# A decode layer's forward heads by pairs: 2 MB cache loads, half-array sums and a shorter softmax loop

## The chip, the cores and the metric

The kernel runs on one core of a Trainium2 chip. The metric is the device time of one execution in microseconds (us): the median of the runs, 1684.61 us for the kernel before (three runs, 1684.12 to 1685.03). A core has five engines that work from their own queues: TensorE (PE; its weight loads are shown as PEld), VectorE (DVE), ScalarE (ACT), GpSimd (POOL) and SyncE (SP), which here issues nearly all the DMAs. Sixteen DMA engines move the data.

## The reference

One decode layer, forward and backward. With B = 4, H = 32, Sk = 4096, Dh = 128, D = 512, F = 1792, all bf16:

```
q   = layernorm(x) @ wq                      # [B, H, 1, Dh]
p   = softmax(q @ k_cache^T / sqrt(Dh))      # [B, H, 1, Sk]
o   = p @ v_cache
h   = x + o @ wo
out = h + (silu(ln(h) @ w1) * (ln(h) @ w3)) @ w2
returned: out and the gradients of x, k_cache, v_cache, wq, wo, w1, w3, w2 for a given grad_out
```

There are 128 heads (batch times head). Each has a K and a V of 4096 x 128 bf16, 1 MB each, so each cache holds 134 MB. The forward part reads both, the backward part reads V again and writes gradients of the size of both.

## The kernel before, in words

**Memory.** One arena of 23 slots of 1 MB (128 partitions x 8320 bytes) holds everything large. `Slot` takes a free one, `give` returns it to the end of the free list. A load into a slot is issued by SP at its place in the program, and waits there for whoever used the slot last.

**Forward part** (to about 665 us). A head's K lies as [partition p, 32 rows j, 128]: partition p holds 32 neighbouring positions, 8 KB. The loop at the end of the diff runs over 64 groups `gi` of G = 2 heads, a = 2 gi and a + 1. The order in each engine's queue is the order of the program text. In one group:

- `S_head` (L393): scores of both heads into one PSUM tile of 128 x 256. Heads take different rows, and quarters c of the array's columns work on quarters of the sequence.
- `sm_max`, `sm_max_T`, `sm_gmax`, `sm_bcast`, `sm_exp`, `sm_sum`, `sm_norm`, `sm_P`: the softmax. The maximum over a row on VectorE (mx, L400), a mask that puts -1e30 in rows of the other head (mxm, L402), a transpose on PE (x_ps, L407), the maximum for each head (gm, L412), its broadcast back by a matmul (b_ps, L417), a copy to SBUF on VectorE (nm, L422), the exponential on ACT (L425), the sum over rows by a matmul (l_ps, L431), the reciprocal (rl, L436), the scaling on ACT (Pn, L439), eight transposes (pt_P, L446) and four copies into P_all (L450).
- For the next group, K is transposed: a quarter on PE with a copy on ACT (`T_pe`, L361, L362), three quarters on VectorE (`T_dve`, L367). POOL prepares W, the masked queries (`q_stationaries`, L373).
- `PK_pairs` (POOL, L456) and `PK_mul` (VectorE, L460): the product of K with the head's probabilities, into a slot PK with two extra columns that hold p itself.
- `M_mm` (L475): 32 steps of a full-array matmul, lhsT = V rows, rhs = PK rows (130 columns), summed over positions in PSUM. It gives the head's output o and a 128 x 128 matrix that the backward part uses for the gradient of q. It runs two to three heads behind, in pieces between the softmax steps: m1 = a - 3 and m2 = a - 2.
- `M_end` (L485, L489): the sums of PK over positions for 32 heads collect in one PSUM tile kP; the head's M is copied by ACT into a slot that holds 16 heads and stays taken until the backward part.
- `kP_flush` after every 32nd head: an ACT copy of kP (L496), four products (L499) and a copy (L500), at once. `O_cols` after every 16th head: two small VectorE copies of the outputs (L505, L507).

K is loaded up to seven heads ahead (`more_K`), V three (`load_V`), each by one DMA of 1 MB. In the last groups `weights` loads the middle part's weights with what slots are left (`reserve`).

**Middle part** (to about 720 us): the rest of the layer forward, and backward to the gradient of o. **Backward part**: heads 0 to 31 one by one, heads 32 to 127 by 48 pairs. A pair is two heads of one batch entry, s and s + 4, in one DMA of 2 MB: partitions 0 to 63 hold the first head, 64 to 127 the second, 64 positions (16 KB) in each partition. The outer products for the gradients of K and V are at L820 and L1434. The probabilities, which the forward part leaves in the layout of single heads, are regrouped for pairs by PE and ACT (`P_rows`).

Of the kernel before, what the change touches and what calls it, by code (L numbers as in the profile page):

```python
# [15 lines left out]
G = 2  # L16
VQ = 3
# [7 lines left out]
LEAD = 64  # L25


@with_exitstack
def kernel(
# [81 lines left out]
    part = {"B": False, "side_done": False}  # L111
# [14 lines left out]
    class Slot:  # L126
        def __init__(self, name, src=free):
            self.i = src[0]
            if part["B"] and src is free:
                lone = sorted((i for i in free if i not in part["pairs"]), key=age, reverse=True)  # L130
                self.i = lone[0] if name in SIDE or lone and age(lone[0]) >= OLD else max(free, key=age)
# [44 lines left out]
    Ks, Vs, KTs, PKs = {}, {}, {}, {}  # L176

    def load_K(s):
        if s < NH:
            Ks[s] = Slot("Kn")  # L180
            nc.sync.dma_start(out=Ks[s].heads(), in_=cache_head(A_k_cache, s))

    nvl = {"n": 0}

    def load_V(s):
        if s < NH and s >= nvl["n"]:
            nvl["n"] = s + 1
            Vs[s] = Slot("Vn")
            nc.sync.dma_start(out=Vs[s].heads(), in_=cache_head(A_v_cache, s))


    def more_K(s):
        while len(Ks) + kdone["n"] < min(NH, s + 8) and len(free) > 1:
            load_K(len(Ks) + kdone["n"])

    kdone = {"n": 0}
    more_K(0)
# [6 lines left out]
    ones_f = const.tile([P, P], FP32, name="ones_f")  # L204
    nc.gpsimd.memset(ones_f[:], 1.0)
# [10 lines left out]

    def ones_window(col):
        i = col % 2
        return onesw[i][:, 32 - i - col:64 - i - col]
# [3 lines left out]
    rowg = fcon.tile([P, 8], FP32, name="rowg")  # L223
    nc.vector.tensor_reduce(out=rowg[:], in_=ident_f.rearrange("p (c g q) -> p g c q", c=4, q=4), axis=AX.XY, op=ALU.add)
    quad = fcon.tile([P, 4], FP32, name="quad")
    nc.vector.tensor_reduce(out=quad[:], in_=ident_f.rearrange("p (q i) -> p q i", q=4), axis=AX.X, op=ALU.add)
    bsum = fcon.tile([P, P], FP32, name="bsum")
    nc.vector.tensor_copy(out=bsum.rearrange("p (c g q) -> p c g q", c=4, q=4),
                          in_=rowg[:, None, :, None].to_broadcast([P, 4, 8, 4]))
    maskneg = fcon.tile([P, G], FP32, name="maskneg")  # L230
    nc.vector.tensor_scalar(out=maskneg[:], in0=rowg[:, 0:G], scalar1=-1.0, scalar2=1e30, op0=ALU.add, op1=ALU.mult)
    wmask = fcon.tile([P, G, 32], BF16, name="wmask")
    nc.gpsimd.memset(wmask[:], 0.0)
    for g in range(G):
        nc.vector.tensor_copy(out=wmask[:, g, 4 * g:4 * g + 4], in_=quad[:])
    selg = fcon.tile([G, P], FP32, name="selg")
# [63 lines left out]
    with ExitStack() as c0:  # L300
        ps0 = c0.enter_context(tc.tile_pool(name="ps0", bufs=1, space=bass.MemoryType.PSUM))
        sg = ps0.tile([G, P], FP32, name="sg_ps")
        nc.tensor.transpose(sg[:], rowg[:, 0:G], ident_f[:])
# [65 lines left out]
    def q_stationaries(gi):  # L369
        W = fw.tile([P, G, 4, 32], BF16, name="W", tag="W", bufs=1)  # L370
        for hl in range(G):
            s = gi * G + hl
            nc.gpsimd.tensor_tensor(out=W[:, hl], in0=qrep[:, :, s:s + 1].to_broadcast([P, 4, 32]),  # L373
                                    in1=wmask[:, hl, None, :].to_broadcast([P, 4, 32]), op=ALU.mult)
# [3 lines left out]
    def S_head(gi, hl):  # L378
# [6 lines left out]
        for k in range(4):  # L385
            for c in range(4):
                if c < NPE:
                    lhsT = zq_window(zq[hl], 4 * hl + k)
# [8 lines left out]
    def sm_max(gi):  # L397
        st = hold[gi]
        mx = fw.tile([P, 1], FP32, tag="mx", name="mx")
        nc.vector.tensor_reduce(out=mx[:], in_=st["S"][:], axis=AX.X, op=ALU.max)  # L400
        st["mxm"] = fw.tile([P, G], FP32, tag="mxm", name="mxm")
        nc.vector.tensor_scalar(out=st["mxm"][:], in0=maskneg[:], scalar1=mx[:], scalar2=None, op0=ALU.add)  # L402

    def sm_max_T(gi):
        st = hold[gi]
        st["x"] = psX.tile([P, 512], FP32, tag="x", name="x_ps")
        nc.tensor.transpose(st["x"][0:G, 0:P], st["mxm"][:], ident_f[:])  # L407

    def sm_gmax(gi):
        st = hold[gi]  # L410
        st["gm"] = fw.tile([G, 1], FP32, tag="gm", name="gm")
        nc.vector.tensor_reduce(out=st["gm"][:], in_=st["x"][0:G, 0:P], axis=AX.X, op=ALU.max)  # L412

    def sm_bcast(gi):
        st = hold[gi]
        st["b"] = psX.tile([P, 512], FP32, tag="x", name="b_ps")
        nc.tensor.matmul(st["b"][:, 0:1], lhsT=selg[:], rhs=st["gm"][:], start=True, stop=True)  # L417

    def sm_exp(gi):
        st = hold[gi]  # L420
        nm = fw.tile([P, 1], FP32, tag="nm", name="nm")
        nc.vector.tensor_copy(out=nm[:], in_=st["b"][:, 0:1])  # L422
# [19 lines left out]
    def sm_P(gi):  # L442
# [4 lines left out]
        v = pt.rearrange("p jj (c g q) -> p g c jj q", c=4, q=4)  # L447
        for q in range(4):
            r_ = slice(32 * q, 32 * (q + 1))
            nc.scalar.copy(out=P_all[r_, gi * G:(gi + 1) * G, :].rearrange("p g (c jj) -> p g c jj", c=4),  # L450
                           in_=v[r_, 0:G, :, :, q])
# [6 lines left out]
    def PK_mul(s):  # L458
# [8 lines left out]
        kdone["n"] += 1  # L467

    def M_mm(s, j0, j1):
        if j0 == 0:  # L470
            hold["M"] = psM.tile([P, PKW], FP32, name="M_ps", tag="M")
        PK = PKs[s].w[:].rearrange("p (j c) -> p j c", c=PKW)
        Vn = Vs[s].heads()
        for j in range(j0, j1):
            nc.tensor.matmul(hold["M"][:], lhsT=Vn[:, j, :], rhs=PK[:, j, :], start=(j == 0), stop=(j == SJ - 1))  # L475

    def M_end(s):
        w = s % 32
        PK = PKs[s].w[:].rearrange("p (j c) -> p j c", c=PKW)
        if w == 0:  # L480
            hold["kP"] = psK.tile([P, 4, Dh], FP32, name="kP_ps", tag="kP")
        for c in range(2):
            for q in range(4):
                j0 = (c * 4 + q) * 4
                nc.tensor.matmul(hold["kP"][32 * q:32 * (q + 1), :, :], lhsT=ones_window(w), rhs=PK[:, j0:j0 + 4, 0:Dh],  # L485
                                 start=(w == 0 and c == 0), stop=(w == 31 and c == 1), tile_position=(0, 32 * q))
        if s % MC == 0:
            Ms.append(Slot("M"))
        nc.scalar.copy(out=M_of(s), in_=hold["M"][:, 0:Dh + 1])  # L489
# [3 lines left out]
    def kP_flush(s):  # L493
        ks = Slot("kP_sb")
# [1086 lines left out]
```

## Time and profile before

| what | before |
|---|---|
| median of the runs | 1684.61 us (1684.12 to 1685.03) |
| profiled execution: its time, its span | 1683.33 us, 1681.5 us |
| busy: PE, VectorE, ACT, POOL | 1243.9, 1238.8, 957.5, 412.9 us |
| HBM read, written | 422.59 MB, 282.34 MB |
| mean rate over the span | 419 GB/s |
| DMA packets | 80983 |
| V loads of 2 MB in the backward part, issue to landing | 31.7 us (median of 48) |
| K loads of 1 MB in the forward part, issue to landing | 15.5 us (median of 128) |

The span is the profiled execution from its first to its last instruction; its own time has 1.8 us more around it. Busy times overlap, so a share of the span says how full an engine is and not what it costs. The page cuts the span into 40 slices of 42 us; digits are busy tenths, and GB/s is what the DMA engines moved. In a timeline, a row gives the start, the length, the engine, the line, the operation with its tiles, how many instructions were merged, and in brackets the idle time before it with what ended it.

### The profile page before, as it was taken

Reading aid. Unit: us, or ns where it says so; the run is one execution under the profiler, and the core shown is the slowest. Engines: PE = TensorE matmul, PEld = TensorE weight load, DVE = VectorE, ACT = ScalarE, POOL = GpSimd, SP = SyncE. Lnnn points to the kernel's source line nnn. Section 1 sums busy time; section 2 is a strip of 40 time slices with the busy share of each in tenths; the row PEclk is TensorE's granted clock in tenths of the full one; section 3 lists DMA queues with packets and bytes.
Section 4 is the critical chain, followed back from the end, with each engine's and each line's share of the span. In section 5 each row is a group of like instructions: output and inputs, shape, how many; then the busy total and the mean of one; then the engine's idle time right before and its main releaser. Section 6 shows DMA issues by size and latency. Waiting matters only on the chain.

```text
span 1681.5 us, 33231 instructions
## 1 busy us (share of the span) xinstructions
PE 1243.9 (74%) x13784; PEld 874.1 (52%) x13784; DVE 1238.8 (74%) x1204; ACT 957.5 (57%) x1482; POOL 412.9 (25%) x732
## 2 busy tenths in 40 slices
PE   5889888888888888877777657567766776776750
PEld 4777776667666776644433335444444443444430
DVE  5989899999999987767766467576655656655682
ACT  3455454445445544677666556666665676676650
POOL 1221222222232223444552323211100011111110
PEclk9999999999999999999999878886667667676675
DMA  9999999999999999999999999999999999999996
GB/s 401 424 425 425 425 424 425 424 425 424 418 424 412 424 404 407 412 409 425 426 426 428 430 430 429 429 430 430 430 430 429 431 429 431 430 429 429 431 431 277
DMA packets 80983, 707.16 MB, mean 421 GB/s; under 512 B 8748, under 2 KB 12984, under 8 KB 15296
## 3 DMA queue, kind: packets, MB, share of 16 engines
q1 hardware_dynamic: 80416, 704.94, 99.4%
q8 instruction: 108, 1.77, 0.4%
q14 instruction: 43, 0.35, 0.0%
q0 software_dynamic: 416, 0.10, 0.0%
HBM read 422.59 MB, written 282.34 MB: 419 GB/s over the span
## 4 chain that ended last, share of the span: by engine, by line
DMA 40%; DVE 8%; PE 5%; ACT 4%; issue 3%; POOL 2%; DVEq 0%; SPq 0%; ACTq 0%; POOLq 0%
DMA out_dram<-arena 37%; DVE arena L1434 6%; ACT arena L806 3%; DMA arena<-in_A_v_cache_dram 3%; POOL zd L1246 1%; PE pt_tps L805 1%; PE M_ps L475 1%; DVE arena L460 1%; PE dq_ps L1032 1%; PE dP_ps L1280 1%; DMA arena<-arena 0%; PE pt_wo L613 0%; POOL P L1251 0%; ACT Pn L439 0%; POOL arena L1431 0%
## 5 line engine op out<-in xcount | busy, mean ns | idle before, releaser
L806 ACT COPY arena<-pt_tps 128x1024 bf16<-128x1024 bf16 x512 | 491.1, 1026 | 239.2 <-PE pt_tps L805 236.1
L805 PE MATMUL pt_tps<-ident_f,arena 128*128 128x128 f32 x2048 | 397.0, 346 | 195.4 <-DMA arena<-in_A_v_cache_dram 111.7
L805 PEld LDWEIGHTS pt_tps<-ident_f,arena 128*128 128x128 f32 x2048 | 290.8, 175 | 362.7 <-issue 187.3
L1434 DVE TENSOR_TENSOR arena<-arena 128x8192 bf16<-128x8192 bf16 x48 | 212.4, 4425 | 206.6 <-DMA out_dram<-arena 176.3
L475 PE MATMUL M_ps<-arena 128*128 128x130 bf16 x4096 | 285.9, 222 | 43.7 <-DMA arena<-in_A_v_cache_dram 43.2
L460 DVE TENSOR_TENSOR arena<-arena 128x4096 bf16<-128x4096 bf16 x128 | 292.4, 2285 | 24.3 <-POOL arena L456 24.3
L475 PEld LDWEIGHTS <-arena 128*128 128x128 bf16 x4096 | 252.3, 99 | 65.1 <-DMA arena<-in_A_v_cache_dram 58.1
L1434 DVE TENSOR_TENSOR arena<-dS,arena 128x8192 bf16<-128x8192 bf16 x48 | 212.4, 4426 | 63.6 <-DMA out_dram<-arena 63.6
L367 DVE STREAM_TRANSPOSE arena<-arena 128x512 f32<-128x512 f32 (+1 forms) x321 | 250.5, 796 | 0.0
L362 ACT COPY arena<-pt_tps 128x1024 bf16<-128x1024 bf16 x128 | 129.4, 1012 | 189.4 <-PE pt_tps L361 147.4
L373 POOL TENSOR_TENSOR W<-qrep,wmask 128x128 bf16<-128x128 bf16 x128 | 120.0, 938 | 85.6 <-PE S_ps L393 71.2
L1431 POOL COPY arena<-arena 128x128 bf16<-128x128 bf16 x48 | 45.2, 941 | 374.5 <-DVE arena L1434 248.6
L456 POOL COPY arena<-P_all 128x64 bf16<-128x64 bf16 x128 | 32.4, 253 | 413.1 <-ACT P_all L450 410.0
L1343 POOL COPY arena<-arena 64x4 bf16<-64x4 bf16 x96 | 78.5, 818 | 127.7 <-PE dP_ps L1363 118.2
L1363 PE MATMUL dP_ps<-arena 128*32 128x512 bf16 x768 | 85.3, 478 | 8.4 <-ACT arena L806 7.9
L450 ACT COPY P_all<-pt_P 32x64 bf16<-32x64 bf16 x256 | 51.9, 203 | 54.6 <-PE pt_P L446 52.4
L820 DVE TENSOR_TENSOR arena<-dS,arena 128x4096 bf16<-128x4096 bf16 x32 | 73.3, 2292 | 12.7 <-DMA out_dram<-arena 12.3
L361 PE MATMUL pt_tps<-ident_b,arena 128*128 128x128 bf16 x1024 | 80.5, 223 | 0.0
L820 DVE TENSOR_TENSOR arena<-P,arena 128x4096 bf16<-128x4096 bf16 x29 | 66.4, 2293 | 18.4 <-DMA out_dram<-arena 17.3
L485 PE MATMUL kP_ps<-arena,onesw 128*32 128x512 bf16 x1024 | 79.6, 388 | 0.0
L393 PE MATMUL S_ps<-arena,W 128*32 128x256 bf16 x1536 | 75.2, 286 | 0.5 <-DVE arena L367 0.2
L439 ACT ACTIVATE Pn<-E,rl 128x1024 bf16<-128x1024 f32 x64 | 73.7, 1151 | 3.2 <-DVE rl L436 3.2
(257 smaller groups left out, 1402.3 us busy)
## 6 DMA issues: line engine op xcount, KB each, us to landing
out_dram<-arena SPq DMA_DIRECT2D x96, 2048.0 KB, 27.5
arena<-in_A_v_cache_dram SPq DMA_DIRECT2D x160, 1024.0 KB, 15.9
arena<-in_A_k_cache_dram SPq DMA_DIRECT2D x128, 1024.0 KB, 15.5
arena<-in_A_v_cache_dram SPq DMA_DIRECT2D x48, 2048.0 KB, 31.7
out_dram<-arena SPq DMA_DIRECT2D x72, 1024.0 KB, 19.8
arena<-in_A_wq_dram SPq DMA_DIRECT2D x8, 1024.0 KB, 17.8
arena<-in_B_w_dram SPq DMA_DIRECT2D x8, 896.0 KB, 14.9
out_dram<-arena SPq DMA_DIRECT2D x6, 896.0 KB, 26.5
```

The lines of the kernel that those rows point to most:

```text
L361: nc.tensor.transpose(pt[:, i, :], Kn[:, c * GW + i, :], ident_b[:])
L362: nc.scalar.copy(out=KT[:, c * GW:(c + 1) * GW, :], in_=pt[:])
L367: nc.vector.transpose(out=KT[:, c * w_:(c + n) * w_], in_=Kn[:, c * w_:(c + n) * w_])
L373: nc.gpsimd.tensor_tensor(out=W[:, hl], in0=qrep[:, :, s:s + 1].to_broadcast([P, 4, 32]), in1=wmask[:, hl, None, :].to_broadcast([P, 4, 32 ...
L460: nc.vector.tensor_tensor(out=PK[:, :, 0:Dh].rearrange("p j (r t) -> p j r t", t=2), in0=Ks[s].heads().rearrange("p j (r t) -> p j r t", t=2),
L475: nc.tensor.matmul(hold["M"][:], lhsT=Vn[:, j, :], rhs=PK[:, j, :], start=(j == 0), stop=(j == SJ - 1))
L485: nc.tensor.matmul(hold["kP"][32 * q:32 * (q + 1), :, :], lhsT=ones_window(w), rhs=PK[:, j0:j0 + 4, 0:Dh], start=(w == 0 and c == 0), stop ...
L805: nc.tensor.transpose(ptw[:, jj, :], w[:, 4 * g + jj, :], ident_f[:])
L806: nc.scalar.copy(out=v.rearrange("p (j d) -> p j d", d=Dh)[:, g * GW:(g + 1) * GW, :], in_=pt[:])
L820: nc.vector.tensor_tensor(out=dst.rearrange("p j (r t) -> p j r t", t=2), in0=col2[:, :, None, :].to_broadcast([P, SJ, Dh // 2, 2]), in1=r ...
L1363: nc.tensor.matmul(rows["acc"][32 * c:32 * (c + 1), :], lhsT=zt[t % B][:, k, ZP - m:ZP - m + 32], rhs=words_of(v, 2 * c + u, k), start=(pl ...
L1434: nc.vector.tensor_tensor(out=dst.rearrange("p (j r t) -> p j r t", r=Dh // 2, t=2), in0=col2[:, :, None, :].to_broadcast([P, 2 * SJ, Dh / ...
```

## The change

- Heads are treated as **units**. Below 32 and from 112 on a unit is a head as before. From 32 to 111 (NPF = 40 pairs) units n and n + 1 are the two halves, by position, of a pair of heads laid out as in the backward part: one DMA of 2 MB into two neighbouring slots (`Twin`). Each unit holds half the positions of both heads. The twin's slots are returned together, when both units are done. Units below 32 also take a twin, with two DMAs of 1 MB.
- Loads are one list in a fixed order (K two pairs ahead of V), issued by `more` whenever enough slots are free; a reserve by place in the group and group number is kept back. Single slots are taken where the neighbour is not free.
- In a paired unit each M step is two matmuls on rows 0 to 63 and 64 to 127 of the array, into two PSUM tiles (both buffers of psM). Both sums are copied after the second unit.
- The score rows are numbered by `row_of`, so that the softmax sums by class; POOL's W is two products of 64 x 256.
- The softmax has no mask step: one row of maxima is transposed, reduced for both heads, and broadcast by two accumulating matmuls; nm is copied by ACT.
- `T_pe(nb)` moves ahead of `sm_max_T`; two VectorE transposes of na become one.
- `kP_flush` is cut in two: the copy stays, the products (`kP_turn`) come at the end of the group and use psX. `O_cols` moves to the end of the group and to POOL.
- In the backward part, pairs below NPF read P_all as it is, and `P_rows` leaves them out. `ones_f` is made in the middle part.

```diff
+RES = (2, 2, 1, 1, 1)
+NPF = 40
...
+            if part["F"]:
+                self.i = next((i for i in src if i ^ 1 not in src), src[-1])
...
+    UP = SP + 2 * NPF
+    def pair_unit(n):
+        return SP <= n < UP
...
+        def __init__(self):
+            self.i = min(self.choices())[1]
+            free.remove(self.i)
+            free.remove(self.i + 1)
+            self.t = arena[:, self.i * SLOT + LEAD:self.i * SLOT + LEAD + 2 * SJ * Dh]
+            self.left = 2
...
+        if pair_unit(n):
+            nc.sync.dma_start(out=tw.t, in_=two_heads(ap, (n - SP) // 2))
+        else:
+            for k in range(2):
+                nc.sync.dma_start(out=of[n + k].heads(), in_=cache_head(ap, n + k))
+    loads = deque()
+    for n in range(0, NH + 4, 2):
+        for of, name, ap, m in ((Ks, "Kn", A_k_cache, n), (Vs, "Vn", A_v_cache, n - 4)):
...
+    def more(reserve):
+        while loads:
+            wide = loads[0][3] < UP
+            if len(free) < reserve + 1 + wide or wide and not Twin.choices():
+                break
+            load_units(*loads.popleft())
...
+    def row_of(paired, hl, q):
+        return 4 * hl + q if paired else 4 * (q // 2) + 2 * hl + q % 2
...
+        if pair_unit(gi * G):
+            for a, s in enumerate(pair_heads((gi * G - SP) // 2)):
+                r_ = slice(64 * a, 64 * (a + 1))
+                nc.gpsimd.tensor_tensor(out=W[r_], in0=qrep[r_, None, :, s:s + 1].to_broadcast([64, G, 4, 32]),
+                                        in1=wmask[1][r_, :, None, :].to_broadcast([64, G, 4, 32]), op=ALU.mult)
...
-        st["mxm"] = fw.tile([P, G], FP32, tag="mxm", name="mxm")
-        nc.vector.tensor_scalar(out=st["mxm"][:], in0=maskneg[:], scalar1=mx[:], scalar2=None, op0=ALU.add)
...
-        nc.tensor.transpose(st["x"][0:G, 0:P], st["mxm"][:], ident_f[:])
+        nc.tensor.transpose(st["x"][0:1, 0:P], st["mx"][:], ident_f[:])
...
-        nc.tensor.matmul(st["b"][:, 0:1], lhsT=selg[:], rhs=st["gm"][:], start=True, stop=True)
+        for g in range(G):
+            nc.tensor.matmul(st["b"][:, 0:1], lhsT=selg[:, g, :], rhs=st["gm"][:, g:g + 1], start=(g == 0), stop=(g == G - 1))
...
-        nc.vector.tensor_copy(out=nm[:], in_=st["b"][:, 0:1])
+        nc.scalar.copy(out=nm[:], in_=st["b"][:, 0:1])
...
+            if pr:
+                for a in range(2):
+                    r_ = slice(64 * a, 64 * (a + 1))
+                    nc.tensor.matmul(hold["M"][a][:], lhsT=Vn[r_, j, :], rhs=PK[r_, j, :], start=(s % 2 == 0 and j == 0),
+                                     stop=(s % 2 == 1 and j == SJ - 1), tile_position=(64 * a, 0))
...
+    def kP_copy():
+        hold["ks"] = Slot("kP_sb")
+        nc.scalar.copy(out=hold["ks"].f(4 * Dh).rearrange("p (c d) -> p c d", c=4), in_=hold["kP"][:])
...
-        kt_ps = psM.tile([P, PKW], FP32, tag="M", name="kt_ps")
+        kt_ps = psX.tile([P, 512], FP32, tag="x", name="kt_ps")
...
+    def weights(gi, k=0):
+        more(reserve.get(gi, RES[k] + (2, 3, 4)[gi] if gi < 3 else RES[k] + (gi % 8 in (1, 2)) + (gi % 16 == 1)))
...
             T_pe(na)
             T_dve(na, 1)
+            T_pe(nb)
         sm_max_T(gi)
...
-            T_dve(na, 2)
+            T_dve(na, 2, 2)
         sm_exp(gi)
         if has1:
             M_end(m1)
-            load_V(m1 + VQ)
+            weights(gi, 1)
             if m1 % 32 == 31:
-                kP_flush(m1)
-            if m1 % MC == MC - 1 and m1 < NH - 1:
-                O_cols(m1 - MC + 1, m1 + 1)
+                kP_copy()
         if hasp:
             PK_pairs(pk1)
         if nxt:
-            T_dve(na, 3)
-            T_pe(nb)
             T_dve(nb, 1)
...
         PK_mul(a)
-        more_K(a + 1)
-        weights(gi)
+        if m1 % MC == MC - 1 and 0 < m1 < NH - 1:
+            O_cols(m1 - MC + 1, m1 + 1, nc.gpsimd)
+        if "ks" in hold:
+            kP_turn(m1)
+        weights(gi, 4)
...
         def P_two(t, n=2):
+            if t < NPF:
+                return P_all[:, SP + 2 * t:SP + 2 * (t + n), :].rearrange("p (t h) j -> p t (h j)", h=2)
```

## The prediction

> **What bounds the kernel now.** I read the page's 40 slices first, then the table of stages, then the order of time of two forward groups.
>
> ```profile
> DVE  5989899999999987767766467576655656655682
> ...
> DMA  9999999999999999999999999999999999999996
> GB/s 401 424 425 425 425 424 425 424 425 424 418 424 412 424 404 407 412 409 425 426 426 428 430 430 429 429 430 430 430 430 429 431 429 431 430 429 429 431 431 277
> ```
>
> The DMA engines are busy in every slice. They move 424 to 425 GB/s in the forward part (slices 2 to 10, loads of 1 MB only) and 429 to 431 in the last two fifths (loads and stores of 2 MB). So the time is about bytes over rate, plus the slices that fall below it. VectorE is at nine tenths or more from slice 6 to 14: it stands close behind the DMA in the forward part.
>
> The stages, with columns: stretch, its us, then PE, PEld, DVE, ACT and POOL busy us (and instructions), granted clock, DMA share, GB/s:
>
> ```profile
> 400.00:440.00 40.00, 34.19 (x570) 27.81 (x567) 37.08 (x51) 19.80 (x45) 10.77 (x24) 1.00 1.01 424
> 440.00:480.00 40.00, 33.40 (x565) 27.61 (x566) 37.42 (x49) 19.48 (x44) 10.71 (x24) 1.00 1.01 417
> ...
> 520.00:560.00 40.00, 34.60 (x576) 28.10 (x574) 37.81 (x49) 20.33 (x46) 10.76 (x24) 1.00 1.00 412
> ...
> 600.00:640.00 40.00, 34.74 (x575) 29.01 (x573) 36.39 (x49) 18.39 (x44) 10.69 (x24) 0.97 0.98 403
> ...
> 1100.00:1200.00 100.00, 71.51 (x384) 45.27 (x385) 66.95 (x40) 64.63 (x81) 14.22 (x19) 0.69 1.01 430
> ```
>
> The nine stretches of 40 us from 80 to 440 us give 424.8 GB/s on average; the six of 100 us from 1000 to 1600 give 429.8. Three dips (417, 412, 403) cost, against 424.8, 0.73, 1.2 and 2.05 us, 4.0 us together. Packet size, not direction, makes the two rates: stretches from 760 to 880 us, with loads and stores of 1 MB, run at 425 to 427.
>
> Now one ordinary group of two heads (timeline; start, us, engine, line, operation):
>
> ```profile
> 633.43 2.29 DVE L460 TENSOR_TENSOR arena<-arena 128x4096 bf16<-128x4096 bf16 x1 [0.29 <-POOL arena L456]
> ...
> 636.10 0.41 DVE L402 TENSOR_SCALAR mxm<-maskneg,mx 128x2 f32<-128x2 f32 x1
> ...
> 637.69 0.38 PE L417 MATMUL b_ps<-gm,selg 2*128 2x1 f32 x2
> ...
> 638.00 0.62 PE L485 MATMUL kP_ps<-arena,onesw 128*32 128x512 bf16 x8
> ...
> 639.22 1.56 PE L475 MATMUL M_ps<-arena 128*128 128x130 bf16 x24
> ...
> 641.84 0.63 PE L475 MATMUL M_ps<-arena 128*128 128x130 bf16 x8
> ...
> 643.22 2.29 DVE L460 TENSOR_TENSOR arena<-arena 128x4096 bf16<-128x4096 bf16 x1 [0.30 <-POOL arena L456]
> ```
>
> From PK_mul(a) to the next PK_mul(a), 633.43 to 643.22, the compute loop takes **9.79 us** with no wait for a load in it. The DMA needs 4 x 2^20 B at 424.8 GB/s, **9.87 us**. Compute is 0.08 us faster, no more. A group in which the K sums are flushed is much longer:
>
> ```profile
> 511.33 2.29 DVE L460 TENSOR_TENSOR arena<-arena 128x4096 bf16<-128x4096 bf16 x1 [0.33 <-POOL arena L456]
> ...
> 517.08 0.17 DVE L505 COPY OT_f<-arena 128x16 f32<-128x16 f32 x1 [0.85 <-ACT arena L489]
> ...
> 517.59 1.08 PE L499 MATMUL kt_ps<-sel_f,arena 128*128 128x32 f32 x8 [1.07 <-ACT arena L496]
> ...
> 523.16 2.29 DVE L460 TENSOR_TENSOR arena<-arena 128x4096 bf16<-128x4096 bf16 x1 [0.33 <-POOL arena L456]
> ```
>
> It takes 11.83 us: VectorE waits 0.85 us for O_cols and PE 1.07 us for the copy of the K sums, each ahead of everything queued behind. At 0.08 us a group, 2 us are not made good, loads are issued late, and the dip of 520 to 560 us follows.
>
> **The change part by part.**
>
> 1. *2 MB loads.* 80 loads (40 of K, 40 of V) take the place of 160: 167.8 MB. At 424.8 GB/s that is 394.9 us, at 429.8 it is 390.3. **-4.6 us**. From below nothing could be gained (if loads alone did not reach the rate of the mixed stretches); from above, 431, the best slice, gives 5.7. I take 4.6. A paired group then needs 9.76 us of DMA; with compute still at 9.79 the gain would be 40 x 0.08 = 3.2.
>
> 2. *The softmax and PE's order.* VectorE loses L402 (0.41), the copy nm (0.16) and one transpose of two (0.69 + 0.69 become 1.24): 0.7 of 9.2 us busy a group. On the loop, by the rows of the group above (T_pe and mx are from the same timeline): T_pe(na) ends at 635.69; T_pe(nb), 0.61, now comes next, so PE reaches the transpose of mx at 636.30 (mx is ready at 636.06) and not at 636.56: -0.26. The broadcast is four instructions instead of two; no row has that, so between 0 and another 0.38 us; I take +0.2. nm goes to ACT: the nearest rows are 0.19 (reading an accumulator, 128x1) against 0.16. So exp starts where it did, 638.33, and l_ps at 638.98. Then Pn no longer stands behind the second KT copy on ACT (1.01 us, from 639.27 to 640.28): after rl it starts at 639.6 and not at 640.18, and ends at 640.75. Between exp and Pn stand two M copies (0.26 each, to 639.42); both PSUM buffers now hold one pair's two sums, so M_mm(m2), which did not wait for them, starts at 639.47 and ends its 24 steps at 641.03. P's transposes start there, against 641.38. Some 0.4 us earlier; the loop is **9.36 us**, if PE's sums cost what they did. It saves nothing by itself, because the DMA (9.76) then ends last; it keeps step 1 whole, and leaves 0.40 us a group.
>
> 3. *Sums of 64 rows.* Each of 64 steps a group becomes two matmuls on two halves of the array. The rows: 24 steps take 1.56 to 1.58 us, 8 take 0.63, so a step is 0.0595 us and a run's end 0.155. No row has row halves. Lower bound 0 (they run abreast); upper bound all in series, 64 x 0.0595 = 3.8 us a group. The nearest rows are matmuls on quarters of the array's columns: eight of L485 with 512 columns each take 0.62. At the full array's pace (0.0595 for 130 columns) one would take 0.23, and eight in series 1.9; so those quarters run abreast. I take **0.1 us** a group, covered by the 0.40.
>
> 4. *Flush and O_cols.* kP_turn moves to the end of the group, with its own PSUM buffer's wait behind P's products; O_cols goes to POOL behind PK_pairs(a), where PK_mul(a) hides it (2.29 us against two copies of 0.17 on VectorE; on POOL up to 0.94 each, the mean of its copies at L1431). kP_copy (0.6 us on ACT) still delays Pn. Of the 2 us a flush group loses I leave 0.6; the loop's slack of 0.3 makes it good in two groups. The dips of 440 and 520 us (1.9 us) shrink to 0.4: **-1.5 us**. The dip of 600 us belongs to unpaired heads with the same reserves: no gain taken; from above it could give 2.
>
> 5. *Slots.* A K pair stays until its second PK_mul, a V pair until its second M_end. Counting slots in program order at group 53 (seven M slots taken): before, K is issued up to a+6 and V up to a-1, 8 MB not yet first used; after, a+5 and a-1, 7 MB. At 430 GB/s that is 17 us, over three transfers of 4.9. Hidden, I take 0; where it is not, one late pair is up to 4.9 us, once or a few times.
>
> 6. *POOL.* W is two products of 64x256 in place of two of 128x128: twice the elements in a row. The pair of rows stands at 1.64 us (while PK_mul runs) and 0.40; doubled at worst +0.8. PK_pairs behind it ends at 636.79, and its reader PK_mul starts at 639.48: 2.7 us of cover. If that were gone, VectorE would wait by what is over. SP issues 80 instructions fewer at 0.33 us; it has slack. The set-up's small VectorE copies lie under the first loads. In the backward part PE and ACT lose the regrouping of P, under the DMA: 0.
>
> Sum: -4.6 - 1.5 = **-6.1 us**. The profiled execution took 1683.33 (span 1681.5 and 1.8 around it), 1.3 below the median of the runs, 1684.61. So 1677.2 for such an execution, and **1678.5** for the median.
>
> [...] In the rows, eight column-tiled matmuls start at 638.00, while the full-width ones before them (637.69, 0.38 long) end at 638.07: a change of tiling cost nothing that is seen. [...]
>
> **The rivals.** *Drains* (slower): six more borders a group, at each end of the M runs against T_pe, the two small products, l_ps and P's transposes, change shape. If each exposes a run's end, 0.155 us, the loop is 9.36 + 0.93 = 10.29, over 9.87 by 0.42; 40 groups make +17: **1702**. It decides once PE grows by over 0.40 us a group, and turns the sign at about 0.6. For it: PE has no idle time left in that loop but for exp. Against: the row at 638.00. Chance 0.11. *In series* (the change does not do what it says): 9.36 + 3.8 = 13.2, 40 x 3.3 = +131: **1816**, and PE over 95% busy. Against it the column quarters. Chance 0.07. *Eaten up*: PE grows by about 0.5, or pairs come late because of the slots, or 2 MB loads alone stay at 425: **1683**, between 1681.3 and 1688. For it: three dips already with 8 MB ahead. Chance 0.16. The forecast, 1675 to 1681, has 0.66; its lower end takes in the dip of 600 us and step 1 at 431.
>
> Faster by over 0.2% (3.4 us, about what a measurement of this kernel can tell from no change): 0.67, counting the border of the third rival; within 0.2%: 0.16; slower: 0.17. The range holds the forecast and the third rival, 0.82: 1674 is the forecast with the rest of the dips (0.4 + 2.05), step 1 at 431 (1.1) and the runs' spread (0.5 either way); 1690 is the third rival's 1688 with half a late pair.
>
> **What would show it.** Step 1: 429 to 430 GB/s in the stretches from 200 to 520 us. Step 2: a PK_mul loop of 9.75 us with PE or VectorE waiting for loads inside it; where it is longer and no load is waited for, PE has become the bound. Step 3: a run of 16 steps near 1.1 us; 2 us would mean in series; a run that starts late after its border means drains. Step 4: no group of 11.8 us, and the dips of 440 and 520 us gone. Step 5: no stretch under 415 before 600 us. The forecast is wrong if the forward part ends later than before, by the first V load of 1 MB in the backward part.

## The result and the profile after

The kernel after takes 1703.6 us (median of four runs, 1701.16 to 1707.24), the kernel before, on the same chip, 1684.36 (1683.97 to 1685.03): a ratio of 1.0116, 95% interval 1.0103 to 1.0128. It is slower by 19 us where 6 us less were forecast. The profiled execution took 1701.16 us, with a span of 1699.4.

The page of the kernel after, its second part (40 slices of 42 us), for the three rows shown of before:

```profile
DVE  5988888788778887577766658576565656555683
...
DMA  9999999999999999999999999999999999999996
GB/s 401 425 425 426 428 428 428 400 407 420 364 352 410 416 401 419 412 405 426 425 427 428 428 430 429 430 430 430 429 430 430 431 429 430 430 430 429 431 429 274
```

VectorE got its relief (8 where 9 stood), and the backward part is as it was. The forward part lost: 428 GB/s in slices five to seven, where paired heads begin, then 352 to 420. By stages of 40 us (stretch, length; busy time and count of PE, PEld, DVE, ACT, POOL; granted clock, DMA share, GB/s):

```profile
200.00:240.00 40.00, 36.72 (x833) 28.96 (x830) 33.06 (x36) 19.91 (x49) 14.29 (x26) 1.00 1.01 427
400.00:440.00 40.00, 36.63 (x792) 29.14 (x780) 31.89 (x36) 18.81 (x44) 12.93 (x23) 0.91 0.99 412
440.00:480.00 40.00, 35.45 (x804) 27.65 (x800) 33.25 (x37) 18.96 (x49) 14.10 (x26) 1.00 0.94 357
520.00:560.00 40.00, 36.72 (x812) 28.92 (x812) 33.47 (x36) 20.33 (x50) 14.07 (x26) 1.00 0.99 408
600.00:640.00 40.00, 36.72 (x693) 29.51 (x693) 35.19 (x37) 20.31 (x49) 11.69 (x27) 1.00 0.98 398
1100.00:1200.00 100.00, 70.11 (x408) 45.80 (x408) 66.62 (x40) 65.90 (x80) 19.64 (x19) 0.73 1.01 430
```

From 440 to 480 us the DMA engines stand idle for part of the time (0.94, where it was 1.01 before). The counts tell more: in the four rows up to 560 us PE has 792 to 833 matmuls in 40 us, before 565 to 576. Three groups follow (timeline; the bracket is the idle time ahead of a row and what ended it):

```profile
400.03 2.25 DVE L553 TENSOR_TENSOR arena<-arena 128x4096 bf16<-128x4096 bf16 x1
...
400.76 1.11 PE L571 MATMUL M_ps<-arena 64*128 64x130 bf16 x32
...
405.71 1.58 PE L571 MATMUL M_ps<-arena 64*128 64x130 bf16 x48
...
407.83 0.64 PE L571 MATMUL M_ps<-arena 64*128 64x130 bf16 x16
...
409.25 2.25 DVE L553 TENSOR_TENSOR arena<-arena 128x4096 bf16<-128x4096 bf16 x1
...
411.76 0.29 PE L571 MATMUL M_ps<-arena 64*128 64x130 bf16 x4 [0.82 <-issue]
...
419.44 2.25 DVE L553 TENSOR_TENSOR arena<-arena 128x4096 bf16<-128x4096 bf16 x1
...
424.95 0.29 PE L571 MATMUL M_ps<-arena 64*128 64x130 bf16 x4 [1.66 <-issue]
...
427.27 2.78 PE L571 MATMUL M_ps<-arena 64*128 64x130 bf16 x48
...
432.87 2.29 DVE L553 TENSOR_TENSOR arena<-arena 128x4096 bf16<-128x4096 bf16 x1 [1.99 <-PE kP_ps L585]
```

The first group, 400.03 to 409.25, is the forecast come true: 32 half-array matmuls in 1.11 us, 48 in 1.58, a loop of 9.22 us. The second takes 10.19 us: PE stops for 0.82 us *inside* a run of 32, after 28, with the same operand tiles as before the stop. "issue" is time in which the engine waits for nothing that the profile shows. The third takes 13.43: after a stop of 1.66 us the run of 48 takes 2.78 us instead of 1.58, because the granted clock has fallen, to 0.50 in this window:

```profile
428.00:432.00 4.00, 4.00 (x66) 3.41 (x66) 2.89 (x2) 1.60 (x5) 0.00 (x0) 0.50 1.02 430
```

PE's waits from 200 to 560 us (what waited, for whom: us in total, times, longest):

```profile
PE M_ps L571 <- issue: 15.5, 20, 1.7
...
PE S_ps L485 <- issue: 6.6, 3, 3.0
PE pt_tps L445 <- issue: 4.0, 4, 1.6
...
PE M_ps L571 <- DMA arena<-in_A_v_cache_dram: 0.3, 1, 0.3
...
PE l_ps L523 <- issue: 0.3, 1, 0.3
```

That is 26.4 us of stops without a releaser, and 0.3 us of waits for V. The kernel before has no stop of that kind there and waits for its loads instead:

```profile
PE M_ps L475 <- DMA arena<-in_A_v_cache_dram: 27.6, 43, 1.7
...
```

So in this stretch the bound has gone from the loads to PE. The chain that ended last agrees: PE has 27% of the span, before 5%.

What do the stops wait for? The queue named "instruction" in the view of the DMA queues, 200 to 560 us (packets, MB, share of 16 engines), with the window's row, of before and then of after:

```profile
q8 instruction: 40, 0.66, 0.6%
```

```profile
200.00:560.00 360.00, 306.50 (x5110) 252.11 (x5108) 335.12 (x441) 178.01 (x402) 96.11 (x216) 1.00 1.01 422
```

```profile
q8 instruction: 55, 0.90, 0.9%
```

```profile
200.00:560.00 360.00, 321.20 (x7095) 254.08 (x7095) 291.51 (x307) 170.15 (x417) 112.47 (x215) 0.97 0.98 402
```

A packet has 16.4 KB. In these 360 us PE and PEld together have 10218 instructions before and 14190 after: 255 and 258 to a packet. PE's program thus comes here in blocks of about 256 instructions while it runs, and a block lasts 360 / 40 = 9.0 us before, and 360 / 55 = 6.5 us after, stops included.

The places of the stops say the same. From 160 to 680 us there are 33, and from one to the next PE always runs a multiple of 128 matmuls, to within two: that is a multiple of 256 instructions, as each matmul has a weight load here (the page of the kernel after counts 16453 of both; 256 matmuls, two blocks, lie between the stops at 411.76 and 424.95 us above). And each time PE goes on 1.2 to 1.6 us after a packet of this queue has landed.

**Theory.** A half-array step is two matmuls and two weight loads in place of one and one, which is 128 PE instructions more a group. Counted in the timeline, a paired group has 414, an unpaired one of the kernel after 286, and a group of the kernel before 282. A fetch that has to pass among the loads isn't back in time for blocks so short, and PE stops at the border of a block. **Rivals:** the tiling drains PE at its borders; the loads by pairs (their slots, their size) are what is late.

### The profile page after: what moved, and what is told of

Its sections match the earlier page's. It is cut to its first block, busy times and chain, and to the rows that moved or that the text cites. A ratio compares the mean times of both kernels' runs of the same rounds, so it can differ in the third digit from the quotient of the medians.

```text
span 1699.4 us, 38125 instructions
## 1 busy us (share of the span) xinstructions
PE 1287.3 (76%) x16453; PEld 897.2 (53%) x16453; DVE 1194.7 (70%) x1018; ACT 962.0 (57%) x1541; POOL 452.3 (27%) x753
## 4 chain that ended last, share of the span: by engine, by line
DMA 43%; PE 27%; ACT 9%; DVE 8%; issue 4%; POOL 2%; DVEq 0%; SPq 0%; ACTq 0%; POOLq 0%
DMA out_dram<-arena 27%; DMA arena<-in_A_v_cache_dram 10%; PE M_ps L571 9%; ACT arena L910 6%; DMA arena<-in_A_k_cache_dram 6%; DVE arena L1536 6%; PE pt_tps L445 3%; PE S_ps L485 2%; PE pt_tps L909 2%; PE pt_P L538 1%; PE b_ps L509 1%; PE kP_ps L585 1%; ACT E L517 1%; PE dq_ps L1136 1%; DVE arena L553 1%
## 5 line engine op out<-in xcount | busy, mean ns | idle before, releaser
L451 DVE STREAM_TRANSPOSE arena<-arena 128x512 f32<-128x512 f32 (+1 forms) x258 | 239.7, 947 | 1.2 <-DMA arena<-in_A_k_cache_dram 1.2
L571 PE MATMUL M_ps<-arena 64*128 64x130 bf16 x5120 | 187.8, 221 | 18.5 <-issue 17.1
L571 PEld LDWEIGHTS <-arena 64*128 64x128 bf16 x5120 | 155.3, 96 | 42.5 <-issue 34.3
L1441 POOL COPY arena<-arena 64x4 bf16<-64x4 bf16 x96 | 95.6, 996 | 129.1 <-PE dP_ps L1461 119.6
L574 PE MATMUL M_ps<-arena 128*128 128x130 bf16 x1536 | 105.2, 220 | 0.0
L458 POOL TENSOR_TENSOR W<-qrep,wmask 64x256 bf16<-64x256 bf16 x80 | 90.8, 1135 | 47.2 <-PE S_ps L485 44.0
L1533 POOL COPY arena<-P_all 128x128 bf16<-128x128 bf16 x40 | 31.9, 797 | 251.8 <-DVE arena L1536 250.9
L574 PEld LDWEIGHTS <-arena 128*128 128x128 bf16 x1536 | 94.3, 99 | 6.1 <-issue 5.9
L445 PE MATMUL pt_tps<-ident_b,arena 128*128 128x128 bf16 x1024 | 75.0, 227 | 14.4 <-DMA arena<-in_A_k_cache_dram 8.7
## 6 DMA issues: line engine op xcount, KB each, us to landing
arena<-in_B_w_dram SPq DMA_DIRECT2D x8, 896.0 KB, 11.4
```

The source lines that it names most:

```text
L445: nc.tensor.transpose(pt[:, i, :], Kn[:, c * GW + i, :], ident_b[:])
L451: nc.vector.transpose(out=KT[:, c * w_:(c + n) * w_], in_=Kn[:, c * w_:(c + n) * w_])
L458: nc.gpsimd.tensor_tensor(out=W[r_], in0=qrep[r_, None, :, s:s + 1].to_broadcast([64, G, 4, 32]), in1=wmask[1][r_, :, None, :].to_broadcas ...
L571: nc.tensor.matmul(hold["M"][a][:], lhsT=Vn[r_, j, :], rhs=PK[r_, j, :], start=(s % 2 == 0 and j == 0), stop=(s % 2 == 1 and j == SJ - 1), ...
L574: nc.tensor.matmul(hold["M"][0][:], lhsT=Vn[:, j, :], rhs=PK[:, j, :], start=(j == 0), stop=(j == SJ - 1))
L1441: nc.gpsimd.tensor_copy(out=zt[t % B][r_, :, ZP + 2 * i:ZP + 2 * i + 2], in_=zt[B][r_, :, s - SP:s2 - SP + 1:B])
```

## The experiments

Each ran beside the kernel before, whose median was 1684.2 to 1684.4 in all series. The edits are to the kernel after.

**1. Which half of the change costs?** Four kernels make a square: pairs or not, half-array steps or not.

```diff
# whole rows
-for a in range(2): matmul(hold["M"][a][:], lhsT=Vn[r_, j, :], rhs=PK[r_, j, :], ..., tile_position=(64 * a, 0))
+matmul(hold["M"][0][:], lhsT=Vn[:, j, :], rhs=PK[:, j, :], ...)
# two 1 MB DMAs
-dma_start(out=tw.t, in_=two_heads(...))
+for k in range(2): dma_start(out=of[n + k].b(), in_=both[:, k * SJ * Dh:(k + 1) * SJ * Dh])
# no pairs
-NPF = 40
+NPF = 0
# halves alone: no pairs, and
+pr = 32 <= s < 112
```

Whole rows:

> The changed kernel with one full-array matmul for each M step in paired units (no row halves; the two heads' sums run together, so the outputs that depend on them are not the reference's). 2 MB loads, twins and order stay. Supply theory (the doubled PE instructions run out between instruction fetches): PE's idle time that ends in issue, about 27 us in the changed kernel from 200 to 560 us, goes to under 2; the loop follows the DMA at about 9.76 us; 1676 to 1680 us. Slot theory (twins hold slots too long, so loads come late): 1700 to 1706, dips at 320 to 520 us stay. Drain theory (changes of tiling shape cost): the changes at six borders go too, so as the supply theory in the time, but PE's pauses would have stood at the borders of the runs and not inside them.

Two 1 MB DMAs a pair:

> The changed kernel with each 2 MB load cut into two of 1 MB with 8 KB rows, into the same twin. Row halves, twins and order stay. Supply theory: PE's issue pauses stay, 15 to 30 us from 200 to 560 us; the rate can reach 425 at most; 1700 to 1708. If the pauses need packets of 16 KB ahead of the fetches, they shrink to under 10 us and the time to 1684 to 1692. Slot theory: 1703 to 1712, since rate is lost too and slots are held as long.

No pairs:

> The changed kernel with NPF = 0: no pair in the forward part, all else of the change (softmax, deferred products, load list) stays. Supply theory: no issue pauses, a compute loop of 9.3 us without waits for loads, so the DMA's 9.87 holds; the dips of the kernel before at 440 and 520 us go; 1681 to 1684. Slot theory: the same, 1681 to 1685, since singles free slots sooner. It prices the rest of the change: -1 to -3.5 us against before.

Halves alone:

> As the run without pairs, but the M steps of heads 32 to 111 are row halves in two PSUM tiles each, of which the second is left out of the output. 1 MB loads into single slots. Supply theory: issue pauses as in the changed kernel, 15 to 30 us from 200 to 560 us, and 1690 to 1706 us. Slot theory: as the run without pairs, 1681 to 1686, no pauses that move the end. Drain theory: a loop of 9.3 to 10.3 us without pauses inside the M runs, 1683 to 1702.

| kernel | time, us | ratio to before (95%) | stops "issue", 200 to 560 us |
|---|---|---|---|
| no pairs | 1683.4 | 0.9994 (0.9985 to 1.0004) | none |
| whole rows (2 MB loads only) | 1680.6 | 0.9980 (0.9970 to 0.9989) | none |
| halves alone (1 MB loads) | 1687.7 | 1.0021 (1.0011 to 1.0031) | 19.0 us |
| two 1 MB DMAs a pair, halves | 1692.9 | 1.0051 (1.0036 to 1.0066) | 24.2 us |
| after: 2 MB loads, halves | 1703.6 | 1.0116 (1.0103 to 1.0128) | 26.4 us |

The 2 MB loads and the new slots cost nothing by themselves; they gain 2.8 us. The stops are there with half-array steps and only with them, at either size of load. Three of the times missed the supply theory's range: whole rows (1676 to 1680), halves alone (1690 to 1706) and two DMAs (1700 to 1708). Halves alone lies in the range of the drain theory, but most of its stops are inside the M runs.

The parts don't add: halves cost 4.3 us with single loads and 23 with pairs. Take the 40 groups of heads 32 to 111, from PK_mul to PK_mul. Without pairs they take 400.0 us, of which PE waits 29.1 for loads; with halves alone 405.0, with 20.4 us of stops and 3.4 of waits. So the stops mostly take the place of waits. In the kernel after the waits are used up too (1.9 us), but the stops are longer, 29.5 us, and the clock is halved for 20.5 us (3.4 with halves alone), of which about half is lost, an estimate from the run of 48 above (2.78 us for 1.58): the groups take 419.3 us. Why pairs lengthen the stops and lower the clock is open.

**2. The steps or their number?** Every second step of the paired units is left out, so that a paired group has 286 PE instructions again; row halves, both PSUM tiles and all borders stay. The three kernels of run 3 free four slots by keeping M in bf16, 32 heads to a slot; their edit is shown here too.

```diff
-for j in range(j0, j1):
+for j in range(j0, j1, 1 + pr):
# bf16 M
+MS = 32
-return Ms[s // MC].w[:].bitcast(FP32)...
+return Ms[s // MS].w[:]...
```

> The changed kernel with every second M step of the paired units left out (row halves stay; outputs that use M and o are not the reference's). PE's instructions a paired group fall from 414 to 286, as in the kernel before. Supply theory: the issue pauses go from 26 us (200 to 560 us) to under 2 us although the halves and all borders between tiling shapes stay; 1678 to 1682 us, near the run with whole rows (1680.6). Drain theory: borders cost what they did; the loop stays over 9.8 us; 1690 to 1702.

1681.7 us (ratio 0.9987, 0.9978 to 0.9996), no stop from 200 to 560 us, 40 packets of instructions. With all borders of tiling in place the loss is gone. Since PE also has less to do here, which could hide a cost of the borders, this run alone neither proves the supply nor refutes *drains*; run 4 does both without leaving any instruction out.

**3. The slots?** Whole rows with bf16 M, the kernel after with bf16 M, and no pairs with bf16 M:

> The run with whole rows, with M kept in bf16: 32 heads in a slot instead of 16, so four slots fewer are taken at the end of the forward part. Slot theory for what was left of the gain (409 GB/s from 440 to 560 us with no pause of PE): that stretch goes to 424 or more; 1674 to 1677.5 us. If slots are not what made it: 1680 to 1681, dip unchanged.

> The changed kernel with M in bf16, 32 heads a slot. Pauses make PE the bound (9.1 us of loop and 0.75 of pauses a group): then slots change little, 1696 to 1704. Pauses are dear only because a late load finds no slots in hand: 1683 to 1692, with 26 us of pauses still there from 200 to 560 us.

> The run without pairs, with M in bf16. All theories: the dips of 440 to 640 us shrink; 1679.5 to 1682.5. A candidate for a version that beats both.

1680.7 (0.9980, 0.9970 to 0.9989), 1700.5 (1.0095, 1.0079 to 1.0112) and 1683.5 us (0.9996, 0.9987 to 1.0006). Four more slots may be worth 3 us to the kernel after, whose four executions alone lie 6 us apart, and nothing to the others; no pairs with bf16 M missed its range of 1679.5 to 1682.5. Why nothing is seen without pairs is told by the windows of no pairs, then of no pairs with bf16 M:

```profile
520.00:560.00 40.00, 35.66 (x579) 29.04 (x582) 33.71 (x36) 20.38 (x48) 11.56 (x25) 1.00 1.00 412
640.00:680.00 40.00, 36.33 (x556) 27.93 (x549) 24.89 (x34) 17.32 (x39) 14.33 (x46) 0.98 1.01 393
```

```profile
520.00:560.00 40.00, 35.69 (x583) 29.00 (x586) 33.77 (x36) 20.50 (x49) 11.47 (x24) 1.00 1.01 425
640.00:680.00 40.00, 36.11 (x547) 27.91 (x540) 24.30 (x34) 16.87 (x37) 16.11 (x46) 0.95 0.94 364
```

The dip of 520 us goes, so it was one of slots. What was loaded early is then lacking at 640 us, where the forward part ends and the DMA engines are no longer full (0.94): the gain is given back later.

**4. Does the fetch wait for the loads?** The paired loads read only half of their bytes; PE's program stays as it is.

```diff
-dma_start(out=tw.t, in_=two_heads(ap, (n - SP) // 2))
+dma_start(out=tw.t[:, 0:SJ * Dh], in_=two_heads(ap, (n - SP) // 2)[:, 0:SJ * Dh])
```

> The kernel after, in which each 2 MB load of a pair of heads reads only the first 8 KB of every partition's 16 KB, so that half of the K and V of heads 32 to 111 is not read (the products use what lies in the slot); all instructions of the engines and their order stay. 80 loads of 2 MB become 1 MB each: 84 MB less, so the loads of that stage need about half their time. Where do TensorE's stops for its next instructions come from? Theory A, the fetch of a block of TensorE instructions waits in the DMA engines behind the packets of the loads: with loads that leave the DMA engines idle for a third of the time or more the stops nearly vanish (under 5 us in 200 to 560 us, against 26.4), a group takes the 9.1 to 9.3 us of the undisturbed loop, 40 groups some 370 us against 419, and the whole about 1703 - 50 = 1650 to 1660 us. Rival B, the fetch has a length of its own that the loads don't set: the stops stay (20 us or more in 200 to 560 us, groups of 10 us or more), and the time stays over 1685. Rival C, the half-array sums themselves hold TensorE up: as B in time, but with stops that lie only at M_ps.

1653.5 us (0.9817, 0.9801 to 0.9834). The window of 200 to 560 us, its queue of instructions and PE's waits:

```profile
200.00:560.00 360.00, 347.73 (x8031) 277.77 (x8029) 326.65 (x349) 193.81 (x472) 130.00 (x241) 1.00 0.64 228
```

```profile
q8 instruction: 62, 1.02, 1.1%
```

```profile
PE l_ps L523 <- ACT E L517: 11.3, 38, 0.3
PE pt_tps L445 <- issue: 0.7, 1, 0.7
PE M_ps L571 <- issue: 0.2, 1, 0.2
```

With the DMA engines 64% busy the same instructions run without stops: 0.9 us against 26.4, a loop of 9.20 us (PK_mul at 402.24, 411.44, 420.64), 40 groups in 372.3 us, the full clock, and a block of instructions used up in 360 / 62 = 5.8 us. Beside loads of 228 GB/s a block came every 5.8 us, beside 402 GB/s every 6.5. Half-array steps are no slower than forecast, and as all borders of tiling stand in these loops, *drains* falls. Theory A of this run holds: here it is the loads that delay the instructions. A block's own packet takes 0.93 us (median) in the kernel before and in the kernel after, and is no shorter in this run (62 packets in 1.1% of 16 engines' 360 us, some 1.0 us each), so the delay lies ahead of the packet; where, the traces don't show.

**5. A dose.** Only 24 of the 40 pairs, in blocks of 8 groups:

```diff
-return SP <= n < UP
+return SP <= n < UP and (n - SP) // 16 % 2 == 0
# and the same condition where the backward part picks the layout of P
```

> The kernel after, in which of the heads 32 to 111 only each second block of 16 is paired (24 pairs of 40: heads 32 to 47, 64 to 79, 96 to 111), and the others are single heads with full-array steps, 286 TensorE instructions a group in place of 414. Theory A, a group with half-array steps is short of instructions and the time lost in it is lost for good, since the loads have no slack to catch up with: the loss over single heads (1703.6 - 1683.4 = 20.2) falls with the number of pairs, 20.2 x 24 / 40 = 12, so 1695 (1692 to 1698). Rival B, the stock of loaded slots bridges a block of 8 groups and the single groups fill it again (their loop of 9.2 us against 9.8 of loading): 1682 to 1688.

1689.2 us (1.0025, 1.0016 to 1.0035); stops 11.4 us. Over no pairs that is 5.8 us, 0.24 a pair; with all pairs it is 20.2, 0.50 a pair. It lies between the two theories (12, and 0 to 5), near the second. In the 40 groups PE still waits 10.1 us for loads, against 1.9 with all pairs, so part of the stops again takes the place of such waits. That single groups refill the stock, and that a long unbroken row of starved groups costs more than its share, fits this but is not shown.

**6. Why do two DMAs of 1 MB lose 11 us less than one of 2 MB?** Packets of 8 KB in one DMA; two DMAs cut by partitions; the second half issued first; the halves' places swapped.

```diff
# packets of 8 KB: the second unit of a twin lies 64 bytes further
+HALF = 4096 + 32
# two by rows
+for k in range(2): dma_start(out=tw.t[64 * k:64 * (k + 1)], in_=two_heads(...)[64 * k:64 * (k + 1)])
# second half first (from two 1 MB DMAs)
-for k in range(2):
+for k in (1, 0):
# halves swapped (from two 1 MB DMAs)
+k = k ^ twin.flip
```

> The kernel after, in which the second half of a twin begins 64 bytes later, so that each 2 MB load stays one DMA but each partition's 16 KB are written in two pieces of 8 KB; all else stays. Why did two DMAs of 1 MB with 8 KB rows (1692.9) lose 11 us less than one of 2 MB (1703.6)? Theory A, the length of the packets: a fetch of instructions behind packets of 16 KB takes longer than behind 8 KB (block to block 6.4 us against 6.1), so this kernel comes out with the former, 1690 to 1695, with a rate at most 425 GB/s. Rival B, the number of DMAs (a load of 2 MB lands as a whole, later for its first unit): this kernel stays with the kernel after, 1700 to 1705.

> The kernel after, with each 2 MB load of a pair cut by partitions into two DMAs of 1 MB (partitions 0 to 63, the first head, and 64 to 127, the second), each row still 16 KB. Cut by positions (8 KB rows, the first half being all that the first unit needs) the two DMAs gave 1692.9; one DMA with packets of 8 KB gave 1703.2. What did the cut by positions bring? Theory A, the first unit of a pair can begin when half of the load is there: here each unit needs both DMAs, so nothing of it is left and the time is that of the kernel after, 1700 to 1705. Rival B, two DMAs in place of one, by how the loads share the engines with the fetch of instructions: the time is again 1690 to 1695, with the longest stop of TensorE for instructions under 2 us and at most two half-clock windows, as there.

> The kernel with two DMAs of 1 MB for each pair (cut by positions, 8 KB rows, 1692.9), with the DMA of the second unit issued first. All else stays. Of the 10.7 us between two DMAs and one (1703.6), what is due to what? Theory A, landing: the first unit can begin when its half is there; here it needs the DMA that lands last, so the gain is gone, 1700 to 1705. Theory C, release: the first half can be issued when the first unit of the twin before it is done, a unit earlier than the whole; here the first DMA issued waits for the second unit of the twin before, so this gain too is gone, 1700 to 1705. Rival B, two DMAs in place of one, whatever their order: 1690 to 1695.

> The kernel with two DMAs of 1 MB for each pair (cut by positions, 1692.9), in which each new use of a twin puts its first unit where the second unit of the use before lay. So the first DMA has to wait until the whole twin before is done, as one DMA does, but its unit can still begin when it has landed. Theory A (landing) keeps the gain: 1690 to 1695. Theory C (release) loses it: 1700 to 1705. Rival B (two DMAs, whatever the order) keeps it: 1690 to 1695. With the run that issues the second half first: 1700 to 1705 there and 1690 to 1695 here says A; both slow says C; both fast says B.

- Packets of 8 KB: 1703.2 us (1.0109, 1.0094 to 1.0124). The length of the packets is not it.
- Two by rows: 2017 to 2050 us (1.2022, 1.1967 to 1.2078), which no theory had; last section. It answers nothing on the question.
- Second half first: 1698.3, from 1691.3 to 1704.5 (1.0095, 1.0074 to 1.0115). Halves swapped: 1695.6, from 1691.5 to 1701.6 (1.0069, 1.0046 to 1.0093). Neither lies where a theory put it, and single executions of one kernel lie 10 to 13 us apart. That the starved kernels scatter is a result, but **the difference between one DMA and two stays open.** What the two traces show of it (executions of 1694.4 and 1701.2 us): the 40 groups take 411.2 us with two DMAs and 419.3 with one; the stops in them are 26.3 and 29.5 us, and the clock is halved for 6.8 and 20.5 us, of which about half is lost. So stops and clock cover these 8 us, the clock more than the stops. The fastest trace, second half first at 1691.3 us, has 21.2 us of stops in them and no halved clock. Why the stops and the clock differ isn't shown by one trace of each.

No kernel that computes all outputs beat the kernel before by more than 0.1%: no pairs is the best, within the uncertainty.

## Why the prediction was wrong, point by point

The step that failed is the third, "I take 0.1 us a group, covered by the 0.40". It priced the half-array matmuls by the time that they take in the array, and as array time 0.1 was right: an undisturbed group takes 9.20 us with halves (run 4), and the shortest groups with full rows 9.08 (whole rows, no pairs). It did not price their *number*: 128 more instructions a group, which came through DMA engines that the loads already filled (share 1.01 from 200 to 560 us before). The 40 paired groups take 419.3 us, or 10.48 each, of which waits for loads are 0.05. So PE's loop is some 1.1 us over the 9.36 of step 2, where 0.1 was taken. That is past the 0.40 at which the first rival said that it decides, and past the 0.6 at which the sign turns. Against whole rows (398.4 us) it is **0.52 us a group**.

The 419.3 us can be put together from the traces: the same groups without stops (run 4) make 372.3; stops for instructions 29.5; waits for loads 1.9 and for VectorE 2.2; the clock, halved for 20.5 us, some 10 by the estimate above. That is 416; the rest of 3 us is not assigned. What the stops took from PE the loads didn't make good: SP waits for M_ps, for slots to come free, for 183 of the 360 us from 200 to 560, so each stop sent a next load later, and the share of the DMA fell from 1.01 to 0.98.

1. *2 MB loads, -4.6:* the rate was nearly right where PE keeps up (427 GB/s from 200 to 240 us; 428 with whole rows from 200 to 440); with packets of 8 KB in the same DMAs it is 418 from 200 to 320 us, where the kernel after has 426. The worth was too high: 1683.4 to 1680.6, 2.8 us. With whole rows the rate falls to 409 from 440 to 560 us; with four more slots it is 422 there and falls to 375 from 640 to 680 instead, for the same time. In the kernel after nothing of it is left.
2. *Softmax and order:* right, even better than forecast: 9.08 us undisturbed with full rows against 9.36.
3. *Above.* The upper bound, "all in series", was far off; the true cost came from something that the step didn't list. "Where it is longer and no load is waited for, PE has become the bound" did name the sign to look for.
4. *Flush and O_cols, -1.5:* the flush became cheaper by less than the 1.4 us taken. Its products now fall into the group behind: without pairs the two groups take 10.03 us (509.94 to 519.97) and 10.96, before 11.83 and 9.79. And the dips didn't go: 419 and 412 GB/s at 440 and 520 us without pairs, 417 and 412 before. Four free slots remove them. So the reading that the flush makes the dip was wrong: it was memory, and worth nothing in the end. All of steps 2, 4 and 6 together brought 1.0 us (no pairs), not to be told from none.
5. *Slots, 0:* nearly right; at most 3 us in the kernel after, none elsewhere.
6. *POOL:* nearly right; VectorE waited 3.6 us for PK_pairs from 200 to 560 us.

*Drains* named 1702 with a loop of 10.29 us, and 1703.6 with 10.48 came. That is chance: the borders that it blames all stand in the loops of 9.20 to 9.22 us, and the stops come at multiples of 256 instructions, 27 of the 28 from 200 to 560 us between two matmuls of one line and shape. *In series* is refuted by the first row of 1.11 us. *Eaten up* had the right direction, but let PE grow by about 0.5 only, for 1683, where it grew by some 1.1.

What the borders of the blocks cost, by the runs: nothing at blocks of 9.0 us beside loads of 422 GB/s (before), 0.9 us in 360 at blocks of 5.8 us beside 228 GB/s (run 4), and 26.4 us in 360 beside 402 GB/s (after), where by run 4 a block would last 5.8 us without stops.

## What to carry to other kernels

Count instructions as well as array time: where an edit splits a matmul in two, compare how long 256 instructions of TensorE last before and after (9.0 us without stops in this case, 6.5 with 26.4 us of them in 360), and look in the trace for "issue" stops inside runs of one shape. Here the program came through the same 16 DMA engines as the loads (0.9% of their time from 200 to 560 us), and the time to get a block was not free: 5.8 us sufficed beside 228 GB/s (0.9 us of stops) and did not beside 402 (26.4). And before a dip in the load rate is laid to an engine that waits, free a slot and see whether it goes, and whether the end moves with it (here, without pairs, four more slots took 412 GB/s to 425 at 520 us, and the time went from 1683.4 to 1683.5 us).

## What the runs showed of the hardware that was not expected

- TensorE's program came as 16.4 KB packets, one for 254 to 261 instructions (200 to 560 us; before, after and runs 1, 2, 4, packets of 8 KB and two by rows), and the stops fit an engine whose next block wasn't there: in the kernel after all 33 from 160 to 680 us lie whole blocks apart, to within two matmuls, and end 1.2 to 1.6 us after a packet has landed. Beside 228 GB/s of loads a block came every 5.8 us with 0.9 us of stops in 360; beside 402 GB/s the mean was 6.5 us with 26.4 us of stops.
- Some stops were followed by a lower clock. Of eleven stops over 1 us from 200 to 560 us in the kernel after, the three longest (1.66 to 2.97) were followed by half the clock for 3.4 or 6.8 us: a run of 48 half-array matmuls took 2.78 us after a stop of 1.66, against 1.58. A lower clock came without stops too: with whole rows, which has none, the mean clock of that stretch is 0.96, and with half of the steps, which has none either, 0.89. What lowers it no run shows.
- Matmuls on the two row halves of the array ran abreast: 32 of them took 1.11 us (at 400.76 us after), as long as 16 full-array ones (1.11 us at 634.13 us before), which is 16 pairs of 0.060 us and a run's end of 0.155.
- Loads that each write 64 of the 128 partitions were slow here (231 GB/s), though the one for the other 64 was issued right behind; why, no run shows. The window of the kernel with loads cut by rows:

```profile
320.00:440.00 120.00, 78.70 (x1400) 62.62 (x1399) 57.96 (x60) 32.97 (x81) 22.75 (x44) 0.77 1.01 231
```

The engines are shown as fully busy at 231 GB/s: 1.8 times the engine time for a byte of the kernel after (100.2% of the engines for 83.59 MB in 360 us, against 96.8% for 143.82), in both with rows of 16 KB.
